# Sums of q and k by two engines instead of by transfers for three batches, and a re-planned order, in a two-scale attention kernel with a gated convolution

## The chip, the cores and the metric

The kernel runs on one core of a Trainium2 chip, as one program. The metric is the device time of one execution in microseconds (us); lower is better. Engine names: PE (TensorE matmul), PEld (its weight loads), DVE (VectorE), ACT (ScalarE), POOL (GpSimd), SP (SyncE, which issues most transfers).

## What is computed

Attention over 8 batches of 8 heads, 576 positions, 64 per head, at two scales that are added, then a convolution gate and two projections with 512 x 512 weights:

```
q_d, k_d, v_d = means of q, k, v over groups of 4 positions   # 144 rows
out_d   = softmax(q_d k_d^T / 8) v_d, repeated 4 times
out_loc = softmax(q k^T / 8 where |i - j| < 4) v
x       = out_d + out_loc, heads side by side                  # 576 x 512
gate    = sigmoid(sum over 5 taps of conv_w[k] * x shifted)
result  = (gate * (x @ w_val)) @ w_out
```

Softmax subtracts the row maximum and adds 1e-9 to the sum. Everything is float32; the projections run as three products of high and low parts (lines 1159 to 1161).

## The kernel before

The work is cut into 32 steps p, one for each batch b = p // 4 and pair of heads c = p % 4. A step has two arms. The local arm: `sl` (banded scores on PE, from the tile `qk` that SP loads), `mx`, `sub`, `exp`, `sum`, `rcp`, `norm` on DVE and ACT, `tl` (transposes on PE), their copy `pt` on ACT, and `x` (PE, with the loaded `vw`). The coarse arm: `sd` (PE, scores of sums over four positions, tile `qs`), `cmx`, `cbi`, three `cexp` with bias `cbi`, `cgrd`, `crcp`, `cnorm` on `pd` (DVE, ACT or POOL), `tc` (transposes), copy `pdt`, and `odp` (PE, with sums of v, tile `vs`; in batch 0 with v itself, tile `vg`), copied by ACT into `od`. DVE adds both into `xt` (lines 990). From `xt` come a high and a low part `xhs`, `xls`, and the gate `gp` with four taps on DVE (line 1070). The projections are cut into blocks j of 504 positions: `v{c}.{part}` and `o{c}.{part}` are pieces of three matmuls each; between them DVE gates (`h`), and ACT and DVE or POOL split it into `hhl`. An `out` block is scaled by ACT into one of two `ob` buffers (line 1251) and SP sends it (`out_t`). From step 8 on `sd` does two steps in one.

The sums over four positions of q and k come in one of two ways. `pool` (lines 720 to 746) adds them from the loaded `qk` on DVE or POOL: per step and for each of q and k an addition of 288 elements into `half` (line 733) and one of 144 into `qs` (line 734). `sums_in` (lines 653 to 689) loads the first of four position slices by SP, and POOL issues three transfers that add the others to it in memory (`accum_op`, line 669), each waiting for the one before. The constant `SUMB = 2` gives batches 0 and 1 to the engines, 2 to 7 to transfers. The sums of v for batches 1 to 7 always come by such transfers.

The order on all engines is made by `Planner`: every operation has a duration for each engine that may run it, a due time (`rank`, from a given order of PE's work and shifts in `SHIFT`), and `simulate` then runs a list schedule. Its start times are the order in which instructions are emitted; each engine then runs its list in order, waiting on semaphores only. `ORDER` is the head of PE's order, written as names; behind it `START`, `STEADY` and `DOUBLE` patterns go on (`tensor_order`). `EARLY` is the order of the first transfers on SP. `Transfers` models the queues of SP and POOL, `fetched` the loading of PE's code in pieces of 127 instructions. Matmuls on constants (line 627) keep PE running where the planner expects a gap. [...]

## Time and profile before

| what | value |
|---|---|
| median of 3 runs | 367.86 us (366.77 to 368.74) |
| the profiled execution's own time | 365.61 us |
| its span, first to last instruction | 363.8 us |
| mean granted TensorE clock | 0.999 |
| PE, DVE, ACT, POOL busy | 98%, 86%, 67%, 19% of the span |
| transfers | 69.01 MB; queue q0, POOL's accumulating ones, 17.50 MB |

The span is what the trace covers; 1.8 us of the profiled execution lie around it. "Busy" is the union of an engine's instructions, and a matmul's end is modelled, so that a busy PE may still lose time between two matmuls; idle time before an instruction, and what ended it, is shown in brackets.

### The profile page before, as it was taken

Reading aid. Unit: us, or ns where it says so; the run is one execution under the profiler, and the core shown is the slowest. Engines: PE = TensorE matmul, PEld = TensorE weight load, DVE = VectorE, ACT = ScalarE, POOL = GpSimd, SP = SyncE. Lnnn points to the kernel's source line nnn. Section 1 sums busy time; section 2 is a strip of 40 time slices with the busy share of each in tenths; the row PEclk is TensorE's granted clock in tenths of the full one; section 3 lists DMA queues with packets and bytes.
Section 4 is the critical chain, followed back from the end, with each engine's and each line's share of the span. In section 5 each row is a group of like instructions: output and inputs, shape, how many; then the busy total and the mean of one; then the engine's idle time right before and its main releaser. Section 6 shows DMA issues by size and latency. Waiting matters only on the chain.

```text
span 363.8 us, 14500 instructions
## 1 busy us (share of the span) xinstructions
PE 354.8 (98%) x6233; PEld 286.3 (79%) x6233; DVE 311.5 (86%) x696; ACT 244.1 (67%) x658; POOL 70.3 (19%) x95
## 2 busy tenths in 40 slices
PE   8899999999999999999999999999999999999996
PEld 5678776777877788888888887788878787878995
DVE  4999999999999699999999999999998996870520
ACT  2999998977687658784868577676767685422221
POOL 5013252622131123211312031202100110000000
PEclk9999999999999999999999999999999999999999
DMA  8999989999999977995699869992434012002012
GB/s 278 315 286 307 325 226 212 253 254 262 249 229 272 251 243 206 227 264 194 231 206 245 244 183 250 220 266 86 142 125 133 2 41 82 33 0 90 25 49 82
DMA packets 23152, 69.01 MB, mean 190 GB/s; under 512 B 2864, under 2 KB 8240, under 8 KB 23088
## 3 DMA queue, kind: packets, MB, share of 16 engines
q1 hardware_dynamic: 18192, 50.42, 41.6%
q0 software_dynamic: 4608, 17.50, 26.3%
q8 instruction: 49, 0.80, 1.0%
q10 hardware_dynamic: 288, 0.16, 0.2%
q14 instruction: 15, 0.12, 0.1%
HBM read 58.63 MB, written 9.44 MB: 187 GB/s over the span
## 4 chain that ended last, share of the span: by engine, by line
PE 78%; DMA 10%; ACT 6%; DVE 3%; issue 1%; POOL 0%; DVEq 0%; ACTq 0%; POOLq 0%
PE out L1159 9%; PE out L1161 8%; PE out L1160 8%; PE val L1159 8%; PE val L1161 8%; PE val L1160 8%; DMA vs<-in_vgr 7%; PE odp L1021 6%; PE x L979 5%; PE tl L929 5%; PE sl L772 5%; PE tc L952 5%; PE sd L849 3%; DMA out_t<-ob 2%; PE sl L758 1%
## 5 line engine op out<-in xcount | busy, mean ns | idle before, releaser
L1070 DVE SCALAR_TENSOR_TENSOR gp<-xt,cw,gp 128x576 f32<-128x576 f32 x128 | 103.4, 812 | 3.1 <-ACT gp L1064 2.4
L1159 PE MATMUL val<-xhs,wh_v 128*128 128x504 f32 (+1 forms) x160 | 63.0, 394 | 0.0
L1161 PE MATMUL val<-xls,wh_v 128*128 128x504 f32 (+1 forms) x160 | 59.5, 372 | 0.0
L1160 PE MATMUL val<-xhs,wl_v 128*128 128x504 f32 (+1 forms) x160 | 59.4, 371 | 0.0
L1159 PE MATMUL out<-hhl,wh_o 128*128 128x504 f32 (+1 forms) x144 | 58.6, 407 | 0.1
L1161 PE MATMUL out<-hhl,wh_o 128*128 128x504 f32 (+1 forms) x144 | 54.8, 381 | 0.0
L1160 PE MATMUL out<-hhl,wl_o 128*128 128x504 f32 (+1 forms) x144 | 54.7, 380 | 0.0
L872 ACT ACTIVATE pd<-sd,cbi 112x144 f32<-112x144 f32 x96 | 35.5, 387 | 7.8 <-DVE cbi L865 7.8
L1251 ACT ACTIVATE ob<-out 128x504 f32<-128x504 f32 (+2 forms) x40 | 22.1, 557 | 24.4 <-PE out L1161 15.3
L1207 POOL TENSOR_TENSOR hhl<-h,hhl 128x504 fp32r<-128x504 f32 (+1 forms) x17 | 19.3, 1138 | 98.8 <-ACT pt L934 41.9
L1187 DVE SCALAR_TENSOR_TENSOR h<-gp,val 128x288 f32<-128x288 f32 (+6 forms) x64 | 26.6, 445 | 12.8 <-PE val L1161 12.7
L959 ACT COPY pdt<-tc 72x336 f32<-72x336 f32 x64 | 25.5, 434 | 16.3 <-PE tc L952 16.1
L1201 ACT CAST hhl<-h 128x504 fp32r<-128x504 f32 (+2 forms) x44 | 22.0, 521 | 20.3 <-DVE h L1187 19.6
L1161 PEld LDWEIGHTS val<-xls,wh_v 128*128 128x128 f32 x160 | 30.1, 188 | 5.2
L1159 PEld LDWEIGHTS val<-xhs,wh_v 128*128 128x128 f32 x160 | 30.1, 188 | 4.6 <-issue 0.8
L1160 PEld LDWEIGHTS val<-xhs,wl_v 128*128 128x128 f32 x160 | 30.2, 189 | 3.6
L809 DVE TENSOR_TENSOR pexp<-ex,rs 64x350 f32<-64x350 f32 x61 | 31.6, 518 | 1.3
L1081 ACT ACTIVATE gp<-gp 128x576 f32<-128x576 f32 x32 | 22.2, 694 | 14.1 <-DVE gp L1070 14.1
L934 ACT COPY pt<-tl 128x256 f32<-128x256 f32 (+1 forms) x64 | 25.7, 430 | 8.7 <-PE tl L929 8.4
L1161 PEld LDWEIGHTS out<-hhl,wh_o 128*128 128x128 f32 x144 | 27.1, 188 | 5.5 <-DVE hhl L1207 0.4
L1159 PEld LDWEIGHTS out<-hhl,wh_o 128*128 128x128 f32 x144 | 27.1, 188 | 5.4 <-DVE h L1187 0.5
L1160 PEld LDWEIGHTS out<-hhl,wl_o 128*128 128x128 f32 x144 | 27.2, 189 | 3.4
(97 smaller groups left out, 711.9 us busy)
## 6 DMA issues: line engine op xcount, KB each, us to landing
qk<-in_qk SPq DMA_DIRECT2D x32, 586.0 KB, 6.1
qs<-in_qkr POOLq DMA_DIRECT2D x18, 576.0 KB, 7.7
vw<-in_vw SPq DMA_DIRECT2D x32, 320.0 KB, 5.4
out_t<-ob SPq DMA_DIRECT2D x32, 252.0 KB, 5.2
vs<-in_vgr POOLq DMA_DIRECT2D x21, 320.0 KB, 8.2
qs<-in_qkr SPq DMA_DIRECT2D x6, 576.0 KB, 6.6
vs<-in_vgr SPq DMA_DIRECT2D x7, 320.0 KB, 6.7
raw_v<-in_w_val SPq DMA_DIRECT2D x4, 512.0 KB, 5.5
```

Of the source, the lines that this page charges most:

```text
L809: return eng.tensor_tensor(out=px[r].rearrange("p (m b) k -> p b m k", b=2)[:, :, :, BQ * e : BQ * e + KW], in0=s["ex"][r].rearrange("p (b ...
L872: nc.scalar.activation(out=s["pd"][:, g], in_=s["sd"][:, g], func=AF.Exp, scale=1.0 / 128.0, bias=s["bi"][:, g : g + 1], accum_out=s["csm" ...
L934: nc.scalar.copy(out=s["pt"][:, lo : lo + n], in_=s["tl", u])
L959: nc.scalar.copy(out=s["pdt"][:, kb], in_=s["tc", kb])
L1070: return nc.vector.scalar_tensor_tensor(out=s["gp"], in0=s["xt"][:, k : k + S], scalar=cw[:, c, k : k + 1], in1=s["gp"], op0=ALU.mult, op1 ...
L1081: nc.scalar.activation(out=s["gp"], in_=s["gp"], func=AF.Tanh, scale=0.5)
L1159: nc.tensor.matmul(out=o, lhsT=wh[:, d, col], rhs=his[d], start=d == 0, stop=False)
L1160: nc.tensor.matmul(out=o, lhsT=wl[:, d, col], rhs=his[d], start=False, stop=False)
L1161: nc.tensor.matmul(out=o, lhsT=wh[:, d, col], rhs=los[d], start=False, stop=d == NC - 1)
L1187: nc.vector.scalar_tensor_tensor(out=t["h"][:, cs], in0=st[b * NC + c]["gp"][:, f:e], scalar=1.0, in1=box["o"][:, cs], op0=ALU.add, op1=AL ...
L1201: nc.scalar.copy(out=t["hh"][:, cuts[n]], in_=t["h"][:, cuts[n]])
L1251: nc.scalar.mul(t["ob"][:, cs], box["o"][:, cs], 0.5)
```

## The change

It has four parts. `SUMB = 2` becomes `SUMS = (2, 5)`: transfers sum q and k for batches 2 to 4 only, and batches 5 to 7 go to `pool`, on DVE or POOL. `EARLY`, `ORDER` and `SHIFT` hold other lists; `ORDER` now reaches to `tl0.14`, where it ended at `v0.0.2`. The planner's model of PE's code is a new one: a piece of code is called for some instructions ahead and, if an accumulating transfer is under way, comes after it; `pick_tensor` prefers, after 60 us, work whose code is not late. The planner's duration of `cbi` is 95 for 77, and an accumulating transfer counts as landed 2700 ns after its data, for 1600.

```
-SUMB = 2
+SUMS = (2, 5)
 EARLY = (
-    "qk.0 vw.0 qk.1 raw.0 vg.0 qk2.0 cwf.0 qk.2 vw.1 raw.1 vg.1 raw.2 qk.3 raw.3 vw.2 vg.2 vg.3 qk.4 vw.3 "
+    "qk.0 vw.0 qk.1 raw.0 vg.0 cwf.0 qk.2 vw.1 raw.1 raw.2 vw.6 qk.3 vw.5 vg.1 vg.2 vw.3 vw.2 raw.3 vg.3 "
...
 ORDER = (
...
-    "odp.11 x.10 x.11 tc1.12 v0.0.2"
+    "odp.11 x.10 tl1.12 x.11 tc1.12 tl0.12 v0.0.2 tl1.13 v0.1.2 v0.2.2 v0.3.2 tc0.13 v1.0.2 sl.13 v1.1.2 "
...
-    LANDING = 1600
+    LANDING, WRITTEN = 1600, 2700
...
-    FETCH = ((60000, 6000), (1e9, 4200))
+    CALL = ((60000, 0, 3650), (1e9, 12, 2300))
+    BRING, BEHIND = 2350, 1400
...
                     if t is not None and t <= now:
-                        return k
-                    if t is not None:
+                        late = now > 60000 and self.fetched(k, now, ops[k]["opts"]["PE"], now, dma, keep=False)
+                        if best is None or late < best[0] - 200:
+                            best = late, k
+                        if best[0] <= 200:
+                            return best[1]
+                    elif t is not None:
...
-            if nm == "qs" and b < SUMB:
+            if nm == "qs" and not SUMS[0] <= b < SUMS[1]:
                 continue
...
-        if p >= NC * SUMB:
+        if SUMS[0] <= p // NC < SUMS[1]:
             return
...
-            pooled = [("qe", x) for x in pairs] if p < NC * SUMB else [("qs3", p // NC)]
+            pooled = [("qe", x) for x in pairs] if not SUMS[0] <= p // NC < SUMS[1] else [("qs3", p // NC)]
...
-        op(("cbi", p), "DVE", 77, bias, [("cmx0", p)])
+        op(("cbi", p), "DVE", 95, bias, [("cmx0", p)])
...
+    def brought(self, call, dma):
+        t = call + next(x for until, _, x in self.CALL if call < until)
+        on = list(dma.added[-6:])
...
+        for begin, end in on:
+            if begin < call + self.BEHIND:
+                t = max(t, end)
+        return t + self.BRING
```

What this moves on the engines, at two places. The first is POOL's queue for batches 5 and 6 (`half20_0` is the first addition for q of step 20, `qs6` the tile of batch 6, `hhl3_1` the low part of block 3). Before:

```order
L1207 TENSOR_TENSOR hhl3_0_3409<-h3_0_3382,hhl3_0_3409 128x504
L1207 TENSOR_TENSOR hhl3_1_3482<-h3_1_3465,hhl3_1_3482 128x504
L1207 TENSOR_TENSOR hhl3_2_3590<-h3_2_3561,hhl3_2_3590 128x504
L669 DMA qs6_3493<-in_qkr 128x1152
L669 DMA vs6_3515<-in_vgr 80x1024
L669 DMA qs6_3493<-in_qkr 128x1152
L669 DMA vs6_3515<-in_vgr 80x1024
```

The same place now:

```order
L1246 TENSOR_TENSOR hhl3_0_3411<-h3_0_3384,hhl3_0_3411 128x504
L772 TENSOR_TENSOR half20_0_3491<-qk20_3360 128x288
L1246 TENSOR_TENSOR hhl3_1_3471<-h3_1_3467,hhl3_1_3471 128x504
L773 TENSOR_TENSOR qs5_3490<-half20_0_3491 128x144
L772 TENSOR_TENSOR half20_1_3560<-qk20_3360 128x288
L708 DMA vs6_3525<-in_vgr 80x1024
L773 TENSOR_TENSOR qs5_3490<-half20_1_3560 128x144
L773 TENSOR_TENSOR qs5_3490<-half21_0_3656 128x144
L773 TENSOR_TENSOR qs5_3490<-half21_1_3720 128x144
L708 DMA vs6_3525<-in_vgr 80x1024
```

The accumulating transfers of `qs6` are gone and additions for steps 20 and 21 stand between the low parts and the transfers of `vs6`. Counted over the whole program, of the 48 new additions DVE runs 8 into `half` and 7 into `qs`, POOL 16 and 17; DVE gives up 4 `cnorm` and 2 `norm` halves, ACT takes 3 `cnorm` more.

The second place is PE's queue at the third output block of block 1 (`out1_2`), whose result needs a free `ob` buffer; `out1_0` is the one that used it before. Before:

```order
L1161 MATMUL out1_2_2352<-hhl1_2_2056,wh_o_98 128x504
L929 MATMUL tl11_1_2378<-ident_77,pexp1_81 128x128 x2
L929 MATMUL tl10_0_2384<-ident_77,pexp0_80 128x128 x3
L1159 MATMUL out1_2_2352<-hhl1_3_2176,wh_o_98 128x504
L1160 MATMUL out1_2_2352<-hhl1_3_2176,wl_o_99 128x504
L1161 MATMUL out1_2_2352<-hhl1_3_2176,wh_o_98 128x504
```

Now (the first half of `sl12`, sixteen rows on the mask, is left out):

```order
L1200 MATMUL out1_2_2366<-hhl1_2_2076,wh_o_98 128x504
L968 MATMUL tl11_1_2392<-ident_77,pexp1_81 128x128 x2
...
L811 MATMUL sl12_2396<-qk12_1903 29x35 x40
L968 MATMUL tl10_0_2452<-ident_77,pexp0_80 128x128 x3
L1198 MATMUL out1_2_2366<-hhl1_3_2189,wh_o_98 128x504
L1199 MATMUL out1_2_2366<-hhl1_3_2189,wl_o_99 128x504
L1200 MATMUL out1_2_2366<-hhl1_3_2189,wh_o_98 128x504
```

The scores of step 12, which stood behind the block, now run before its last piece.

## Rows read from the trace of the kernel before

**Rows 1.** The page's first part: busy time, share of the span and instructions of each engine.

```profile
PE 354.8 (98%) x6233; PEld 286.3 (79%) x6233; DVE 311.5 (86%) x696; ACT 244.1 (67%) x658; POOL 70.3 (19%) x95
```

**Rows 2.** Busy time by stretch of the span: start and end in us, length, then for each engine busy us and count, granted clock, share of the DMA engines' time, GB/s.

```profile
10.00:50.00 40.00, 38.46 (x838) 29.78 (x839) 39.47 (x96) 37.51 (x103) 8.62 (x10) 1.00 0.97 302
50.00:100.00 50.00, 49.12 (x839) 37.50 (x838) 48.85 (x104) 39.24 (x106) 18.97 (x23) 1.00 0.99 243
...
170.00:290.00 120.00, 119.52 (x2330) 97.22 (x2329) 114.87 (x263) 84.37 (x238) 20.33 (x20) 1.00 0.65 178
```

**Rows 3.** The waits of PE over the whole span: who waited for whom, us in total, times, longest.

```profile
PE odp L1021 <- DMA vs<-in_vgr: 0.5, 1, 0.5
PE tl L929 <- ACT od L1031: 0.5, 1, 0.5
...
PE odp L1021 <- ACT pt L934: 0.4, 1, 0.4
PE odp L1021 <- issue: 0.4, 1, 0.4
```

**Rows 4.** The chain of waits that ended last, between 113 and 123 us: start, us, what.

```profile
113.55 0.59 ACT ob L1251
...
114.17 7.44 DMA out_t<-ob
...
121.69 0.59 ACT ob L1251
...
122.70 0.71 PE odp L1021 x8
```

**Rows 5.** The timeline of SP's queue, ACT and PE between 227 and 237 us: start, us, engine, line, operation, out<-in; in brackets idle time before it.

```profile
227.72 0.83 SPq L644 DMA_DIRECT2D out_t<-ob  x2
...
235.33 0.59 ACT L1251 ACTIVATE ob<-out 128x504 f32<-128x504 f32 x1 [1.15 <-PE x L979]
235.82 0.70 ACT L1031 COPY od<-odp 128x288 f32<-128x288 f32 x2
...
236.26 0.85 PE L929 MATMUL tl<-ident,pexp 128*128 128x128 f32 x5 [0.45 <-ACT od L1031]
```

**Rows 6.** The page's DMA issues: queue, count, KB each, median us from issue to landing.

```profile
qk<-in_qk SPq DMA_DIRECT2D x32, 586.0 KB, 6.1
qs<-in_qkr POOLq DMA_DIRECT2D x18, 576.0 KB, 7.7
...
out_t<-ob SPq DMA_DIRECT2D x32, 252.0 KB, 5.2
```

**Rows 7.** The additions into `half` and `qs` (duration in ns, least, median, most; first and last start), and two groups of DVE work (count | busy us, mean ns of one | idle before).

```profile
L733 DVE TENSOR_TENSOR half<-qk x12: 404/448/460, 4.9 to 49.9; 128x288 f32<-128x288 f32 x12
L734 DVE TENSOR_TENSOR qs<-half x10: 247/300/308, 5.4 to 60.5; 128x144 f32<-128x144 f32 x10
L734 POOL TENSOR_TENSOR qs<-half x6: 416/425/427, 6.3 to 57.3; 128x144 f32<-128x144 f32 x6
L733 POOL TENSOR_TENSOR half<-qk x4: 659/664/668, 7.5 to 59.7; 128x288 f32<-128x288 f32 x4
...
L809 DVE TENSOR_TENSOR pexp<-ex,rs 64x350 f32<-64x350 f32 x61 | 31.6, 518 | 1.3
...
L897 DVE TENSOR_TENSOR pd<-pd,crs 112x432 f32<-112x432 f32 x16 | 9.7, 613 | 0.2
```

**Rows 8.** DVE instructions that ran beside a POOL addition (timeline: start, us), and the spread of the same two forms over the span (ns, least, median, most).

```profile
67.36 1.07 DVE L865 TENSOR_SCALAR cbi<-cmx 112x3 f32<-112x3 f32 x1
...
172.14 1.03 DVE L1070 SCALAR_TENSOR_TENSOR gp<-xt,cw,gp 128x576 f32<-128x576 f32 x1
...
L865 DVE TENSOR_SCALAR cbi<-cmx x32: 146/155/1189, 8.5 to 289.0; 112x3 f32<-112x3 f32 x32
...
L1070 DVE SCALAR_TENSOR_TENSOR gp<-xt,cw,gp x128: 746/808/1157, 24.3 to 322.5; 128x576 f32<-128x576 f32 x128
```

**Rows 9.** The timeline where the load of `qk` for step 23 is issued by SP, and where the coarse scores of steps 22 and 23 run on PE.

```profile
190.72 0.64 SPq L644 DMA_DIRECT2D qk<-in_qk  x1
...
209.37 0.97 PE L849 MATMUL sd<-qs 64*64 64x144 f32 x24
```

**Rows 10.** The timeline of PE where it goes from a projection's piece to the scores of a step.

```profile
207.91 0.39 PE L1160 MATMUL val<-xhs,wl_v 128*128 128x504 f32 x1
208.14 0.40 PE L1161 MATMUL val<-xls,wh_v 128*128 128x504 f32 x1
208.47 0.27 PE L758 MATMUL sl<-mask_b,ident_b 64*32 64x175 bf16 x8
208.56 0.88 PE L772 MATMUL sl<-qk 64*29 64x35 f32 x80
```

**Rows 11.** The timeline of PE and ACT at the first coarse transposes of steps 4 and 5.

```profile
48.68 1.03 ACT L895 ACTIVATE pd<-pd,crs 112x144 f32<-112x144 f32 x3
48.77 0.35 PE L952 MATMUL tc<-ident,pd 112*72 112x112 f32 x2
...
49.45 0.60 PE L952 MATMUL tc<-ident,pd 112*72 112x112 f32 x2
```

**Rows 12.** The timeline where SP issues the load of v for step 1 (`vg`), and where PE first uses it.

```profile
11.16 0.33 SPq L644 DMA_DIRECT2D vg<-in_vg  x1
...
22.19 0.46 PE L1021 MATMUL odp<-pdt,vg 72*64 72x144 f32 x3
```

## The prediction

> **What bounds the kernel now.** I read the page's busy times first. PE is busy for 98% of the span, DVE for 86%, ACT for 67%, POOL for 19% [rows 1]: PE bounds the whole, and DVE comes near enough to bound a stage. The table by stretches says where. From 10 to 50 us PE is busy 38.46 of 40 us, DVE 39.47 and ACT 37.51, with the DMA engines at 97%; from 50 to 100 us PE has 49.12 of 50. From 170 to 290 us, the stage where batches 5 to 7 are worked on, PE has 119.52 of 120 us and DVE 114.87 [rows 2]. So nearly all that PE can win lies before 100 us, where DVE has no time to spare, and in a few holes behind. The list of PE's waits gives those holes their size: 0.5 us for the accumulated v, 0.5 for ACT's copy `od`, 0.4 for ACT's copy `pt`, 0.4 with no releaser ("issue") [rows 3].

> Two of the holes have one cause. At 113.55 us ACT scales an output block; its transfer takes 7.44 us; ACT stands until 121.69 before it may write that buffer again; the copy `pt` behind it in ACT's queue comes late, and PE starts `odp` at 122.70 [rows 4], after a hole of 0.4 [rows 3]. At 235.33 us it happens again: ACT had been idle for 1.15 us, the output transfers had been issued from 227.72 on, the copy `od` is queued behind, and PE loses 0.45 us [rows 5]. The row names `x` as the releaser there, but scaling an output block doesn't read it; the landing fits, 7.6 us after the issue. The median output transfer lands in 5.2 us [rows 6]. What both moments share is accumulating transfers in the air.

> **The change, part by part.** All terms are against the profiled execution's own 365.61 us; the median of the runs is 367.86, so 2.25 us higher, and I carry the difference over to it.

> *Transfers removed.* Batches 5 to 7 lose 3 plain loads and 9 accumulating transfers of 576 KB. The output transfer of 227.72 us then flies beside transfers of v alone, and at the median of 5.2 us it lands 2.4 us sooner, more than ACT's idle 1.15. PE's hole of 0.45 us closes: **-0.45**, bounds -0.45 and 0.

> *PE's order at block 1.* The transfers of batches 3 and 4 stay, so the output transfer of 114.17 us may stay long. But `sl` of step 12 now runs before the last piece of the third output block, so ACT asks for the buffer later by about the 0.88 us that such scores take (208.56 to 209.44 us, by the starts around it [rows 9, 10]). PE's own hole is 0.4: **-0.4**, bounds -0.4 and 0, since the copies behind ACT's wait could be wanted elsewhere.

> *Fewer steps down to small matmuls.* Behind a projection's piece a matmul of scores starts 0.33 us after the last big one, where a big one follows another in 0.23 [rows 10], so an entry costs 0.1. By PE's two lists there are 7 fewer entries from a `v` or `o` piece into `sl`, `sd`, `x` or `odp`, and 5 more from transposes, whose price no row shows; it lies between 0 and the same 0.1. So -0.7 to -0.2; I take **-0.4**.

> *The early transposes.* At 48.68 us the transposes of step 5 follow those of step 4 and wait, slice by slice, for ACT's three normalizing instructions: two of step 4 take 0.35 us together, two of step 5 0.60 [rows 11]. The change puts nine matmuls and `x` between. Some 0.6 us could go. But PE next needs the accumulated v of batch 1, for which it already waits 0.5 us [rows 3], and that chain of three transfers starts from the same place in SP's list. What PE saves at 49 us it waits for at 56: **0**, bounds -0.6 and +0.5 (the chain later, by the two additions that POOL now runs between its transfers).

> *First loads.* `vg` of step 1 moves behind a weight load of 512 KB and a `qk` of 586 KB, which at the 302 GB/s of that stretch [rows 2] is 3.6 us. Issued at 11.16 us before, it would land at 17.3 with `qk`'s median of 6.1 [rows 6] and now at about 20.9; PE uses it at 22.19 [rows 12]. Covered by 1.3 us: **0**, and up to +1 if the queue is slower. The fourth weight load moves back by three transfers, some 3 us; its first use is over 15 us later.

> *The planner's view of late code.* The 0.4 us of "issue" is the only wait of PE that has no other releaser [rows 3]. A plan that knows when code comes late has little to win here: **0**, bounds -0.4 and +0.5 for a new wait, since scores of steps 13 and 14 now run back to back.

> *The sums.* DVE runs 8 more additions of 0.448 us and 7 of 0.300, and gives up 4 `cnorm` of 0.613 and 2 halves of `norm` of 0.518 [rows 7]: 3.6 + 2.1 - 2.5 - 1.0 = +2.2 us. Its idle time from 170 to 290 us is 120 - 114.87 = 5.1 us [rows 2], which hides it, with 2.9 left. POOL runs 16 of 0.664 and 17 of 0.425, 17.8 us on an engine idle four fifths of the time, and loses 9 issues. Are the sums in time? `qk` of step 23 is issued at 190.72 us; with 6.1 us it lands at 196.8; the two additions for q and two for k take 2.2 us on POOL; the scores run at 209.37 [rows 9]. Ten us of cover, so a transfer of `vs` waited for in POOL's queue ahead of them (7.7 us for one of that kind [rows 6]) still fits. Three `cnorm` more on ACT lie beside work of other engines, since ACT has 84 of 120 us. **0**, if the additions leave DVE's instructions as they are.

> Sum: -0.45 - 0.4 - 0.4 = -1.25, so 364.4 for a profiled execution and **366.6 us** for the median.

> **The rivals.**

> *A, slower: the additions hold DVE up.* A `cbi` that met a POOL addition took 1.07 us, where the median is 0.155, and a tap 1.03 us against 0.808 [rows 8]. So a meeting costs 0.22 to 0.92 us, and I take the middle, 0.57. The stage where 33 more such POOL instructions run has 2.9 us of DVE idle left. For it: the stage holds most of the taps, and additions are tied behind one DVE instruction only. Against it: the plan keeps them apart, and the median tap and `cbi` have their short length although POOL runs low parts beside them already. From six meetings on PE waits; from eight (4.2 / 0.57) the kernel is slower than before. With eleven: 6.3 - 2.9 - 1.25 = +2.1, **370.0**. [...]

> *B, nothing is won.* Before 100 us DVE is busy 98 to 99% of the time [rows 2]; what PE saves there it waits for again, and the two holes behind ACT move to the next output block. Then **367.8**.

> *C, faster: the runs held more of these waits than the profiled execution.* The median lies 2.25 us above it. If that is output blocks and loads waiting beside accumulating transfers, half of it, 1.1 us, may go with those of batches 5 to 7: **365.5**. For it: a transfer took 7.44 us where the median is 5.2. Against it: no row of the other runs is there.

> **How the numbers follow.** About 0.5%, 1.84 us, is what a measurement can tell from no change. Forecast 0.50 (365.2 to 368.0: faster by over that 0.17, within it 0.32, slower 0.01), A 0.18 (slower 0.16, within 0.02), B 0.12 (within 0.11, slower 0.01), C 0.20 (all faster). So faster 0.37, same 0.45, slower 0.18. The range, 364.0 to 370.0, holds the forecast with its bounds, B, nearly all of C and half of A, and leaves out about 0.12.

> **What would show it.** Right: ACT's idle time before an output block near 120 and 235 us gone, and PE's waits for `pt` and `od` with it; DVE busy some 2 us more between 170 and 290 us, with `cbi` near 0.16 us and taps near 0.81; additions done 5 us or more before the scores that use them; PE's wait for `vs` near 56 us still there. Wrong: PE waiting for `qs`, or DVE instructions of batches 5 to 7 over 1 us (A); PE's gaps before 100 us shorter by over 1 us, which I gave nothing; or new "issue" waits near steps 13 and 14.

## The result, and the profile after

The changed kernel takes 369.35 us in the median (365.48 to 370.79), the kernel before beside it 367.44: ratio 1.0054, 95% interval 1.0034 to 1.0074. A second series gave 369.47 against 367.36, ratio 1.0089 [1.0044, 1.0135]. So it is slower, by some 2 us; the forecast was 366.6. The medians here and below are of all executions, while a ratio leaves out those over 1.5% above their kernel's fastest, so that it need not be the ratio of the two medians. The profiled execution took 370.2 us, with a span of 368.2.

The page's first part, two queues of its third and two rows of its last, after:

```profile
PE 357.0 (97%) x6236; PEld 289.2 (79%) x6236; DVE 313.0 (85%) x705; ACT 249.3 (68%) x667; POOL 82.1 (22%) x122
...
q0 software_dynamic: 3312, 12.19, 18.5%
q8 instruction: 49, 0.80, 1.0%
...
out_t<-ob SPq DMA_DIRECT2D x32, 252.0 KB, 2.4
...
qs<-in_qkr POOLq DMA_DIRECT2D x9, 576.0 KB, 7.7
```

The parts that the change meant to move did move: half of the accumulating transfers of q and k are gone, an output block lands in 2.4 us instead of 5.2 [rows 6], POOL has 12 us more work [rows 1]. Now the stretches that answer to [rows 2], and one more:

```profile
10.00:50.00 40.00, 36.53 (x692) 28.64 (x693) 34.94 (x83) 32.83 (x87) 8.83 (x11) 0.91 0.94 285
50.00:100.00 50.00, 48.94 (x966) 37.83 (x966) 49.15 (x109) 40.73 (x108) 16.83 (x20) 1.00 0.96 241
140.00:150.00 10.00, 9.70 (x234) 7.49 (x233) 9.26 (x24) 5.80 (x22) 4.04 (x4) 1.00 0.51 119
170.00:290.00 120.00, 119.88 (x2329) 97.61 (x2330) 117.94 (x274) 86.69 (x238) 32.45 (x48) 1.00 0.51 143
```

From 170 to 290 us PE is as busy as before, 119.88 of 120 us, and DVE is 3.1 us busier, with 2.1 to spare. From 10 to 50 us PE ran 692 matmuls instead of 838, at a granted clock of 0.91, and DVE and ACT, nearly full before, stood idle for 5 and 7 us. The waits of PE, which answer to [rows 3]:

```profile
PE tl L968 <- DVE pexp L848: 1.7, 2, 0.9
PE odp L1060 <- issue: 1.6, 1, 1.6
PE sl L811 <- issue: 1.0, 1, 1.0
...
PE x L666 <- ACT pd L911: 0.4, 1, 0.4
PE out L1198 <- DVE h L1226: 0.3, 1, 0.3
```

The waits for accumulated v, for `od` and for `odp`'s `pt` are gone. "issue", 0.4 us before, is now 2.6. PE's timeline shows its two places (columns as in [rows 10]; in brackets the wait):

```profile
22.26 0.47 PE L1060 MATMUL odp<-pdt,vg 72*64 72x144 f32 x4
24.32 3.62 PE L1060 MATMUL odp<-pdt,vg 72*64 72x144 f32 x28 [1.60 <-issue]
...
70.43 0.65 PE L811 MATMUL sl<-qk 64*29 64x35 f32 x52
72.05 0.35 PE L811 MATMUL sl<-qk 64*29 64x35 f32 x28 [0.97 <-issue]
```

Both stops are in the middle of a group whose operands are all there. What is missing, as I read the records of q8, is code. This queue, of kind `instruction` above, moves 49 transfers of 16 KB (0.80 MB), in before and after alike. Counted from the first, PE's pairs of weight load and matmul can be cut into blocks of 127 (the first has 94), which gives 49 ends as well, and every stop with no releaser of 0.15 us or more, in any trace here, stands 2 to 7 pairs behind the end of such a block: here behind the fourth of 32 `odp`, there behind the 52nd of 80 `sl`. For each end of a block there is one transfer of q8, which starts between 2 us before PE passes that end and 7 us behind it (2.5 and 8.5 in f4, below). That it brings the block after next is read from the stops, since no record names what a transfer holds: PE goes on 1.2 to 1.6 us after it has landed (before 1.43 at 23.01 us, after 1.39 at 24.32 and 1.29 at 72.05, f4 1.54 at 43.30). One stretch of the DMA view, 21.55 to 23.0 us, holds the transfer for the first stop, between loads of SP (from 17.0 to 21.55 us q8 moves nothing):

```profile
q1 hardware_dynamic: 154, 0.35, 91.7%
q8 instruction: 1, 0.02, 5.7%
```

By this reading the margin at each block is the time that PE takes for one block, less the time from a block's end until the code is there and those 1.2 to 1.6 us more. From the traces' records of q8 and of PE's starts, in us:

| profile | end of a block | code of the block after next lands | end of the next block | PE goes on |
|---|---|---|---|---|
| before | 17.00 | 21.58 | 22.20 | 23.01 |
| after | 17.04 | 22.93 | 22.26 | 24.32 |
| before | 62.15 | 64.35 | 66.42 | no stop |
| after | 65.88 | 70.76 | 70.81 | 72.05 |

At 70 us accumulating transfers were in the air from 59 to 72 us, and in the new order PE passes an end of a block, at 65.88, in their midst. That they delay the code isn't shown: in the kernel before such transfers ran from 62.2 to 67.4 us, and the code for the end at 62.15 landed 2.2 us behind it.

### The profile page after: what moved, and what is told of

It is laid out like the page before. It is cut to its first block, busy times and chain, and to the rows that moved or that the text cites. A ratio compares the mean times of both kernels' runs of the same rounds, so it can differ in the third digit from the quotient of the medians.

```text
span 368.2 us, 14558 instructions
## 1 busy us (share of the span) xinstructions
PE 357.0 (97%) x6236; PEld 289.2 (79%) x6236; DVE 313.0 (85%) x705; ACT 249.3 (68%) x667; POOL 82.1 (22%) x122
## 4 chain that ended last, share of the span: by engine, by line
PE 77%; DVE 13%; ACT 4%; issue 3%; DMA 1%; DVEq 0%; ACTq 0%
PE out L1198 8%; PE out L1199 8%; PE out L1200 8%; PE val L1198 7%; PE val L1200 7%; PE val L1199 7%; PE odp L1060 6%; PE sl L811 5%; PE tc L991 5%; PE x L1018 5%; PE tl L968 4%; DVE gp L1109 4%; PE sd L888 3%; DVE h L1226 1%; PE sl L797 1%
## 5 line engine op out<-in xcount | busy, mean ns | idle before, releaser
L1226 DVE SCALAR_TENSOR_TENSOR h<-gp,val 128x288 f32<-128x288 f32 (+6 forms) x64 | 26.6, 445 | 13.2 <-PE val L1200 12.9
L1246 POOL TENSOR_TENSOR hhl<-h,hhl 128x504 fp32r<-128x504 f32 (+1 forms) x18 | 20.1, 1118 | 75.7 <-DVE gp L1109 41.4
L1029 DVE TENSOR_TENSOR xt<-x,od 128x290 f32<-128x290 f32 x64 | 25.7, 446 | 9.3 <-PE x L1018 5.4
L848 DVE TENSOR_TENSOR pexp<-ex,rs 64x350 f32<-64x350 f32 x59 | 30.6, 518 | 1.3
```

The source lines that it names most:

```text
L848: return eng.tensor_tensor(out=px[r].rearrange("p (m b) k -> p b m k", b=2)[:, :, :, BQ * e : BQ * e + KW], in0=s["ex"][r].rearrange("p (b ...
L1029: nc.vector.tensor_tensor(out=s["xt"][:, 4:].rearrange("p (m a j r) -> p a m j r", m=NPR, a=2, r=2)[:, par], in0=s["x"][par].rearrange("p ...
L1226: nc.vector.scalar_tensor_tensor(out=t["h"][:, cs], in0=st[b * NC + c]["gp"][:, f:e], scalar=1.0, in1=box["o"][:, cs], op0=ALU.add, op1=AL ...
```

## Experiments

Theories: (1) the new order of the first loads makes PE's code late before 50 us; (2) PE's new order puts ends of blocks where code comes late; (3) the sums cost nothing. The rival to all was A of the prediction. Where "every list as it is" is said, the planner's choices were replaced by each engine's own list, written out, and only what the text names was altered.

### The sums

s1 and d2 are one kernel, run twice: before, with `SUMS = (2, 5)` and the three conditions on it, planned again. s4: after, with

```diff
-SUMS = (2, 5)
+SUMS = (2, 8)
```

s1: 

> The kernel before with only the sums of q and k for batches 5 to 7 on VectorE and GpSimd (PE's list is the same up to two entries). Theory 3 (the sums are hidden, and an output transfer that finds no accumulating transfers beside it lands sooner): the hole near 236 us gone, 0 to 0.7 us faster than before, 366.7 to 367.4. Rival (the additions on GpSimd hold VectorE up, or DVE runs out of idle time): 1 us or more slower than before, over 368.4, with VectorE's instructions of batches 5 to 7 longer or PE waiting for them.

d2: 

> The kernel before with only the sums of q and k for batches 5 to 7 on VectorE and GpSimd, once more beside the others, since it is the best so far: 0 to 0.4% faster than before if the sums gain what the holes behind output transfers cost, 365.9 to 367.4; the same as before if those holes are chance.

s4: 

> The changed kernel with the sums of q and k of batches 5 to 7 back on accumulating transfers (PE's list the same up to 11 entries behind 250 us). Theory 3: same as the changed kernel or up to 0.7 us slower, 369.3 to 370.0, with the hole near 236 us back. Rival (the sums cost the time): 1 to 2 us faster than the changed kernel, 367.4 to 368.4.

Measured: s1 366.21 us, ratio to before 0.9996 [0.9967, 1.0025]; d2 365.81, 0.9982 [0.9950, 1.0013]; s4 368.40, 1.0040 [1.0011, 1.0069]. By s1 and d2 the sums cost nothing; a gain isn't established. s4 alone would not decide it: its 368.40 lies at the edge of what the rival gave, not in the range of theory 3. In d2, 170 to 290 us reads

```profile
170.00:290.00 120.00, 120.00 (x2341) 97.85 (x2342) 117.02 (x276) 88.05 (x249) 32.83 (x47) 1.00 0.49 138
```

PE has no wait there, and DVE has the 117 us that the prediction worked out. s4, without the sums of batches 5 to 7 on engines, is still slower than before. The slowdown is elsewhere.

### The first loads

f1 and d1 (one kernel, run twice): before, every list as it is, but SP's first 18 loads; f2: after, with the opposite edit.

```diff
-... qk.2 vw.1 raw.1 vg.1 raw.2 qk.3 raw.3 vw.2 vg.2 vg.3 qk.4 vw.3
+... qk.2 vw.1 raw.1 raw.2 qk.3 vg.1 vg.2 vw.3 vw.2 raw.3 vg.3 qk.4
```

f1: 

> The kernel before, every engine's list of instructions as it was, except that SP issues its first 18 loads in the order of the change (raw_v third, qk of step 3 ahead of vg of step 1). Theory 1 (the new order of the first loads makes code and loads late for PE near 20 to 25 us): PE stops for 1 to 1.6 us at odp of step 1, where before the kernel stopped 0.4, in some executions with a stretch at half clock behind it: 1 to 2 us slower than before, 368.5 to 369.5. Theory 2 (the loss is all in PE's own new order, later): same as before, 367.4, stop of 0.4 or less.

d1: 

> The kernel before with SP's first 18 loads in the order of the change, once more, since the first runs gave 1.0038 [1.0006, 1.007] but a profile with no long stop near 24 us. Theory 1: 0.3 to 0.5% slower than before again, and in a second profile a stop or a stretch of lower clock between 10 and 50 us, where it loses 1 us more than before. Rival (the first runs were chance): within 0.2% of before.

f2: 

> The changed kernel, every engine's list as it is, except that SP issues its first 18 loads in the order of before. Theory 1: the stop at odp of step 1 shrinks from 1.6 to 0.4 us and the clock of 20 to 40 us is 1.0; 1.2 to 2 us faster than the changed kernel, 367.3 to 368.2, so about as before. Theory 2: same as the changed kernel, 369.3, with a stop of some 1.6 us still there.

Measured: f1 368.86 us, 1.0038 [1.0006, 1.0070]; d1 368.65, 1.0036 [0.9998, 1.0073]; f2 368.18, 1.0037 [1.0009, 1.0064]. So the loads alone cost some 0.37% (d1's interval just reaches 1), and f2, where they are the old ones, shows that the other new lists cost as much by themselves. That is what theory 1 said of the time, but mostly not of the place: in neither profile does `odp` stop for long at 24 us (f1 0.21 us), and a second profile of the changed kernel itself (a0, below) did not stop there at all. A place that recurs is 35 us, in the scores of step 5. In f1, and in a0:

```profile
34.64 0.23 PE L960 MATMUL sl<-qk 64*29 64x35 f32 x3
35.76 0.43 PE L960 MATMUL sl<-qk 64*29 64x35 f32 x33 [0.89 <-issue]
```

```profile
34.22 0.23 PE L811 MATMUL sl<-qk 64*29 64x35 f32 x5
35.16 0.85 PE L811 MATMUL sl<-qk 64*29 64x35 f32 x75 [0.71 <-issue]
```

Of eight profiles with the new loads (four in flight, blocks where they were) five wait there, 0.4 to 0.9 us, two others (after and f3) at 24 us, 1.6 us; of six with the old loads one waits at 35 us, 0.36 us, and none longer than 0.6 at 24. The block before ends at about 29 us, the next one 5.5 us later. From the end at 29 us until the code lands it takes 4.0 to 4.7 us in the six profiles with the old loads, 4.6 to 5.1 in the six with the new that had not stopped at 24 us. With the new order the four 512 KB loads `raw_o` are issued from 28.3 to 34.5 us in f1, from 28.1 to 32.3 in before: the code goes through beside them.

That these stops are the 0.37% isn't shown. Kernels with the old loads stop too: s1 for 0.72 us at 30 and for 1.00 us at 49 us, c2 (below) for 1.11 us at 18. The stop at 49 us, in the scores of another step, stands in four of the five profiles with the old list of PE and four loads in flight, 0.3 to 1.0 us, with either order of the loads. Here those of s1 and d1:

```profile
48.92 0.63 PE L772 MATMUL sl<-qk 64*29 64x35 f32 x49 [1.00 <-issue]
...
50.45 0.63 PE L960 MATMUL sl<-qk 64*29 64x35 f32 x49 [0.97 <-issue]
```

All stops for code ("issue", 0.15 us or more) before 60 us add up to 0 to 1.9 us in the six profiles with the old loads and to 0.4 to 2.1 in the eight with the new.

g2: f1 with fewer loads in flight; g3: s1 with the same edit; every list as it is.

```diff
-PACE = 4
+PACE = 3
```

g2: 

> The kernel before with the new order of the first 18 loads, and SP holding three loads in flight instead of four. Theory 1 (code for PE waits behind the loads that were issued ahead of it): the code of the block that ends at 29 us lands within 4.3 us of that end instead of 4.8 to 5.1, and the wait of step 5's scores at 35 us is gone; unless loads themselves come late, 0.2 to 0.4% faster than with four in flight, so as before. Rival (the code's delay has nothing to do with the loads in flight): 4.6 us or more, wait still there, time as with four or slower.

g3: 

> The kernel before with the sums of q and k of batches 5 to 7 on VectorE and GpSimd, the best so far (0.9996 and 0.9982 of before in two sessions), with three loads in flight instead of four. Theory 1: its waits for code before 60 us (0.6 to 1.9 us in two profiles) fall below 0.5 us, and it is 0.1 to 0.4% faster than before. Rival: with three in flight qk or vg come late before 60 us, where the DMA engines are 97% busy, and it is 0.3% or more slower than before.

Measured: g2 372.15 us, 1.0143 [1.0104, 1.0181]; g3 373.00, 1.0142 [1.0102, 1.0181]. Neither waits for code in step 5, and the code lands 3.4 us (g2) and 2.6 us (g3) behind the end of that block. But these ends come later, at 31.7 and 33.6 us, and with four loads in flight the code for an end at 33.7 us, in the changed kernel's profile, landed 2.5 us behind it. The first seven blocks together say more: the code landed 3.5 us behind their ends in the mean in g2, where it was 5.1 and 4.9 in f1 and d1, and 2.8 in g3, where it was 5.0 and 4.2 in s1 and d2. So fewer loads in flight go with sooner code. The time is that of g3's rival: PE waits for ACT and DVE instead. That late loads are behind these waits isn't shown: DVE's additions wait for `qk` 8.9 us in g2 (6.0 in f1), but 5.5 in g3 (4.9 in s1). The largest waits of g2:

```profile
PE tc L815 <- ACT pt L1122: 1.7, 2, 1.5
PE tl L1117 <- ACT pdt L1147: 1.6, 1, 1.6
PE x L815 <- DVE ex L975: 1.0, 1, 1.0
PE sd L1037 <- DVE xt L1178: 0.8, 1, 0.8
```

### The ends of blocks

a0 is the changed kernel itself. f4 has 48 pairs more at the start:

```diff
+        for _ in range(52 if plan.warm == 12 else 0):
+            nc.tensor.matmul(out=bank[0:32, 0:8], lhsT=ones(64, 32), rhs=ones(64, 8), ...)
-        for _ in range(plan.warm):
+        for _ in range(8 if plan.warm == 12 else plan.warm):
             nc.tensor.matmul(...)
```

a0: 

> The changed kernel as it is, beside the three below. All theories: 368.8 to 369.8, some 0.5% above before. A second profile tells a stop that belongs to the kernel from one that this execution had by chance: PE's loss from 140 to 150 us (1.4 us, 1.0 more than before) should stand in every profile, since there two blocks of 127 of PE's load and matmul pairs end 3.2 us apart, while the code for the block after next arrives 4.3 to 5 us after a block's end; the 1.6 us at 24 us may not.

f4: 

> The changed kernel, every engine's list as it is, with 48 more load and matmul pairs on PE at the very start (52 of 8 columns in place of 4 of the 12 warm-up matmuls of 350 columns), while PE waits for its first data; so each block of 127 pairs ends 48 pairs earlier in the work. By the trace's start times, ends of blocks then lie 1.5 us apart at 38 us, 1.2 us at 134 us, 3.7 at 78 us, 4.1 and 4.2 near 31 and 33 us. Theory 2: with 4.8 us from the end of a block to the arrival of the code for the block after next, 6.3 us more are lost than in the changed kernel, at those places: 373 to 376. Rival (blocks of code have nothing to do with the stops): the time as the changed kernel's, 369 to 370.5.

Measured: a0 369.47 us, 1.0089 [1.0044, 1.0135]; f4 377.24, 1.0282 [1.0228, 1.0335], 7.8 us more than a0 beside it, just above the 376 expected. The added pairs run while PE had nothing to do, and the first scores start at 5.24 us, as in the changed kernel (5.23). f4's stops stand at ends of blocks: at three of the places worked out beforehand (38, 78 and 134 us by the changed kernel's trace, later here by the stops before them; at 78 us 1.06 us are lost), and at 8 us, which the expectation had not listed:

```profile
7.91 0.63 PE L1013 MATMUL sl<-qk 64*29 64x35 f32 x50
11.59 0.35 PE L1013 MATMUL sl<-qk 64*29 64x35 f32 x30 [3.05 <-issue]
...
39.32 0.91 PE L868 MATMUL tc<-const-bfloat16-1.0 128*72 128x336 bf16 x5
43.30 0.29 PE L1193 MATMUL tc<-ident_s,pd 112*72 112x112 f32 x1 [3.06 <-ACT a_o L1349]
...
138.66 0.77 PE L1013 MATMUL sl<-qk 64*29 64x35 f32 x65
141.21 0.29 PE L1013 MATMUL sl<-qk 64*29 64x35 f32 x15 [1.78 <-issue]
```

The row of 43.30 names ACT's `a_o`, which is not read there; blocks end at 37.69 and 39.20 us, the code lands at 41.76, PE goes on 1.5 us later. So there the releaser in the bracket hides a wait for code. Every other engine's list is the same in f4, so it is shown that here the place of the blocks' ends alone cost 7.8 us.

### PE's order behind 118 us, and at 70 us

In every profile with the whole new list of PE, 140 to 150 us loses 1.3 to 1.6 us beyond what its matmuls take (how that is reckoned stands below, with the other stages; the expectations have 1.4 to 1.6 by slightly other prices); with the list of before, 0.3 or less. Two blocks end 3.2 us apart there; in the changed kernel's profile the code lands 2.3 and 3.6 us behind these two ends, where a0's expectation had 4.3 to 5; at the first seven ends of before it was 3.8 to 5.1. f3 gives PE its old order for steps 13 to 15, with ACT, DVE and POOL planned again; f5 in addition the old loads, planned again too; c1 moves six entries with every other list as it is; c2 also `sl.7` behind two pieces, with the old loads; g1 adds 8 pairs of 8 columns at 118 us.

```diff
 f3, f5: PE's list from v0.1.2 on as in the kernel before
 c1, c2:
-odp.12 odp.13 v3.2.2 tl1.14 v3.3.2 o0.0.2 x.12 x.13
+v3.2.2 v3.3.2 o0.0.2 odp.12 odp.13 tl1.14 x.12 x.13
 c2:
-o0.0.0 tc1.6 sl.7 o1.0.0 o0.1.0
+o0.0.0 tc1.6 o1.0.0 o0.1.0 sl.7
```

f3: 

> The changed kernel with PE's list for steps 13 to 15 as before the change (scores of steps 13 and 14 no longer back to back); SP's list is unchanged, ACT, DVE and GpSimd planned again. The ends of PE's blocks of code then lie 5 us or more apart at 135 to 150 us. Theory 2 (PE's new order brings ends of blocks nearer together than code arrives): the loss from 140 to 150 us falls from 1.4 to 0.5 us; 0.7 to 1.2 us faster than the changed kernel. Rival (the loss there comes from the changed work of DVE and ACT): 1.2 us or more is still lost there, the time as the changed kernel's.

f5: 

> The changed kernel with PE's list for steps 13 to 15 and SP's first 18 loads both as before the change. Theories 1 and 2 together: 1.7 to 2.5 us faster than the changed kernel, as before or up to 0.3% faster than it, 366.5 to 367.6. If only PE's list counts: as the kernel with that list alone; if neither: as the changed kernel.

c1: 

> The changed kernel, every engine's list as it is, but that three pieces of projections (nine matmuls) run between the scores of step 15 and the products of steps 12 and 13 instead of behind them. The two ends of code blocks near 141 and 144 us then lie 5 us apart instead of 3.2. Theory 2: the loss of PE from 140 to 150 us, 1.4 to 1.6 us in the four profiles with that order, falls to 0.5 to 0.8; 0.6 to 1.0 us faster than the changed kernel. Rival (the loss there comes from something else in steps 12 to 15): 1.3 us or more still lost, the time as the changed kernel's.

c2: 

> As the kernel before this one, and in addition two pieces of output projections ahead of the local scores of step 7 (the ends of code blocks near 66 and 71 us then lie some 6 us apart instead of 4.9) and SP's first 18 loads in the order of before. Theories 1 and 2: no wait for code in the scores of step 7 (0.4 to 1.5 us in three of four profiles); 1.5 to 2.5 us faster than the changed kernel, as before or up to 0.3% faster than it. Rival (scores that start 1.4 us later make DVE late, which has no time to spare before 100 us): the wait for code goes, and the transposes of step 7 wait for DVE instead; as the kernel before this one.

g1: 

> The changed kernel, every engine's list as it is, with 8 more load and matmul pairs of 8 columns on PE at 118 us, so that from there on each block of code ends 8 pairs earlier in the work; the ends near 141.1 and 144.3 us come to lie some 4.5 us apart instead of 3.2. If the loss from 140 to 150 us (1.4 to 1.6 us) is code: it falls to 0.9 or less, and the time by 0.3 to 0.7 us against the changed kernel. If it is the chain of copies on ACT and DVE in steps 12 to 15: 1.3 us or more is still lost there and the time is the changed kernel's, or up to 0.4 us more for the pairs.

| | us | ratio to before | lost from 140 to 150 us |
|---|---|---|---|
| f3 | 373.23 | 1.0144 [1.0068, 1.0221] | 1.8 |
| f5 | 371.25 | 1.0143 [1.0086, 1.0200] | 1.3 |
| c1 | 372.05 | 1.0142 [1.0084, 1.0200] | 3.2 |
| c2 | 370.82 | 1.0085 [1.0051, 1.0119] | 3.2 |
| g1 | 370.98 | 1.0107 [1.0065, 1.0148] | 1.5 |

All five missed: none is faster than the changed kernel. Planning the other engines again brought new waits (f3 and f5: `out <- DVE h`, up to 1.5 us). c1 made `odp` 2 us later, counted from the scores of step 15; ACT copies it (`od`) ahead of the exponentials `pd` of steps 14 and 15 in its list, and `x`, which follows them, waited:

```profile
146.06 0.81 PE L1212 MATMUL x<-pt,vw 64*64 64x58 f32 x40
148.12 1.32 PE L1212 MATMUL x<-pt,vw 64*64 64x58 f32 x40 [1.25 <-ACT pd L1105]
```

In g1 the ends lie 4.5 us apart as meant, but the code came 4.1 us after the first instead of 2.3, and two starts of `odp` still lay 0.57 us apart. So at 143 us two starts of `odp` at a block's end lie 0.24 to 0.69 us apart in four of the five profiles with the new order of steps 12 to 15. In the fifth, a0, they do not, and it loses as much: late code is not the larger part here. In after, a0, s4 and f2 some 0.3 to 0.5 us more are lost where an output piece follows transposes (at 150.03 us in the changed kernel's profile, behind DVE's `h`). How the rest divides stays open.

At 70 us the scores of step 7 stop for code in six of eight profiles with that order (0.28 to 1.74 us), in none of five with the order of before. c2, which moved them, does not stop there, but its copies then make it wait 1.05 us for DVE at 68 us: the rival of that expectation.

## Why the prediction was wrong

PE's time beyond what its matmuls take, by stage (worked out from PE's starts: each time between two starts, less the mean of its kind over the nine profiles of the table, outliers left out; matmuls on constants count as lost; us, mean and spread):

| stage | old lists, old loads (before, s1, d2) | old lists, new loads (f1, d1) | new lists, old loads (f2) | new lists, new loads (after, a0, s4) |
|---|---|---|---|---|
| 20 to 50 | 12.3 (12.0 to 12.6) | 12.6 (12.3 to 12.9) | 11.3 | 13.4 (12.5 to 14.8) |
| 50 to 80 | 1.6 (1.5 to 2.0) | 2.0 (1.9 to 2.1) | 2.8 | 2.8 (2.4 to 3.4) |
| of it, matmuls on constants | 0.1 | 0.7 | 0.5 | 1.2 |
| 80 to 140 | 2.5 (2.2 to 3.0) | 2.4 (1.7 to 3.0) | 1.4 | 1.8 (1.2 to 2.8) |
| 140 to 150 | 0.1 (0.0 to 0.3) | 0.2 (0.1 to 0.3) | 1.3 | 1.5 (1.3 to 1.6) |

Against before the last column has +1.1, +1.2, -0.8 and +1.4 us, and +0.2 in all other stages, together some +3.0, as the spans of these profiles (366.8 in the mean against 363.8); the medians of the two series say +1.9 and +2.1. The +1.2 from 50 to 80 us is time of matmuls on constants: three more are in the list, and some that ran at 48 us before now run past 50.

Stops for code, named by "issue", add up to 0.4, 2.5 and 0.6 us over the whole span in before, s1 and d2, to 2.1 and 2.5 in f1 and d1, to 1.9 in f2 and to 2.6, 1.1 and 2.1 in after, a0 and s4. So profiles of one kernel differ as much as the kernels do, and the means (1.2 old, 1.9 new) account for 0.7 of the 3.0 us directly. That the two new lists cost the time is shown by f1, d1 and f2; that late code can cost it, by f4; how much of it late code is, stays open.

- *The planner's view of late code*, put at 0 with bounds -0.4 and +0.5, and with it the order of PE, is the first step that failed. The prediction took the 0.4 us of "issue" [rows 3] for all there was to win or lose. It was the remainder of a margin that one execution of before happened to keep (s1, with PE's list the same up to two entries, stops for 2.5 us): a new order of 6,236 pairs moves every end of a block behind 33 us. Measured: with the old loads, f2, the new lists cost 0.37%, some 1.4 us, where all terms without the loads had come to -1.25. Of that, the stop for code at step 7 is 0.3 to 1.7 us in six of eight profiles, and `odp` at 143 us up to 0.6. The prediction did name new "issue" waits as a sign against it, near steps 13 and 14; the larger one came at step 7.
- *First loads*, put at 0 and up to +1, is the second: 0.37%, some 1.4 us, in f1 and d1. The price was asked of `vg` alone. `vg` itself was in time in f1 and d1, as worked out [rows 12] (in g1 `odp` waited 0.65 us for it, at 23.5 us); PE's code, which no row of [rows 6] lists and which takes time of the same 16 DMA engines as the loads (after, 21.55 to 23.0 us: q8 5.7%, q1 with the loads 91.7%), landed 4.6 to 5.1 us behind the end at 29 us instead of 4.0 to 4.7. How much of the 1.4 us that is stays open.
- *The two holes behind ACT* (-0.45 and -0.4): gone in the changed kernel's profile, and output blocks land in 2.4 us, as in s1 and d2 (s4, with the transfers, 4.6). The hole of 0.4 at 122.70 us stands in three of the five profiles with the old list of PE (s1 and d1 below; not in f1 and d2) and in none of after, a0, s4 and f2, so it was real, but of some executions. The one at 236.26 us stands in no other profile with the accumulating transfers of before (f1, d1); s4 has one like it, 0.79 us, at 201 us. A hole of one execution was counted as one of every execution.

```profile
123.35 0.71 PE L1021 MATMUL odp<-pdt,vs 72*64 72x144 f32 x8 [0.42 <-ACT pt L934]
...
125.21 0.71 PE L1209 MATMUL odp<-pdt,vs 72*64 72x144 f32 x8 [1.03 <-ACT pt L1122]
```

- *Fewer entries* (-0.4): not seen. By the same reckoning the matmuls that are not on constants take 325.2 us in either list.
- *The early transposes* (0): with the old loads 20 to 50 us lost 11.3 us, 1.0 less than before, in one profile. PE now waits for `pexp` near 40 us (0.5 to 1.3 us in all profiles with the new lists) where it waited for `pdt` (0.3 to 0.7). The wait for accumulated v near 56 us, forecast to stay, is gone in the changed kernel's profile and 0.9 us in s4.
- *The sums* (0): right, and rival A is refuted. The signs it asked for are not there: `cbi` and taps keep their median lengths [rows 8], and PE waits for nothing of DVE from 170 to 290 us.

```profile
L904 DVE TENSOR_SCALAR cbi<-cmx x32: 151/159/973, 8.5 to 292.3; 112x3 f32<-112x3 f32 x32
...
L1109 DVE SCALAR_TENSOR_TENSOR gp<-xt,cw,gp x128: 755/808/1192, 24.3 to 326.8; 128x576 f32<-128x576 f32 x128
```

  A's two prices were read beside the wrong instructions. The `cbi` of 67.36 us and the tap of 172.14 us [rows 8] ran beside high and low parts on POOL; the additions of sums end at 60.5 us in that kernel [rows 7]. POOL before, at these times:

```profile
66.17 1.55 POOL L1140 TENSOR_TENSOR wl_o<-a_o,wh_o 128x512 fp32r<-128x512 f32 x1
67.48 0.92 POOL L1207 TENSOR_TENSOR hhl<-h,hhl 128x252 fp32r<-128x252 f32 x1
...
171.31 1.25 POOL L1207 TENSOR_TENSOR hhl<-h,hhl 128x504 fp32r<-128x504 f32 x1 [11.59 <-DVE gp L1070]
```

  In the changed kernel's profile eleven of the two kinds met an addition, as many as A reckoned with: six `cbi` of 0.15 to 0.24 us, but for one of 0.73 that met a low part too, and five taps of 0.80 to 0.85. The longer `cbi`, 0.53 to 0.97 us, and a tap of 1.19 ran beside POOL's parts and normalizations, 0.8 to 1.4 us long. All `cbi` together took 8.7 us, 1.1 more than before, all taps 103.5, 0.4 less. Against the median of 0.159 us, six `cbi` beside POOL's long instructions took 0.4 to 0.8 us more, three others beside such instructions 0.16 to 0.29 us in all; taps beside additions show next to nothing of it (819 ns in the mean, 808 for the others). What holds the six up isn't shown.
- *Rival C* (half of the 2.25 us between median and profile goes): didn't come; the changed kernel's medians lie further up. For the transfers by themselves the intervals of s1 and d2 leave room for it (up to 0.3 and 0.5%).

Lower clocks stand behind the long stops. In the changed kernel's profile the 28 `odp` behind the stop of 1.60 us are 3.62 us long, where 29 took 2.05 before, and 20 to 30 us have a granted clock of 0.72, with 0.50 from 25 to 28; in f4 the stretches of 10 to 20 and 40 to 50 us, with the stops of 3.05 and 3.06 us, have 0.83. Over the timed executions, the mean granted clock was below 0.997 in 8 of 92 of the kernel before, 1 of 24 with the sums alone, 7 of 24 with the new loads alone, 17 of 34 of the changed kernel; its executions above that have a median of 368.3 us, those below 370.2, and those of before above it 367.0. So some 1.3 us of the slowdown stand without a lower clock. That the stops cause the lower clock is my estimate from this order in time (after: stop to 24.32 us, 0.50 from 25 us on); no run shows it.

The best kernel of the study is before with the sums alone (s1, d2): not slower than before, and not shown to be faster.

## What to carry to other kernels

PE is busy here for 97 to 98% of the span and runs 6,233 to 6,236 short pairs, and its code, as read from q8, came in 49 transfers beside the loads. In these traces a wait of 0.15 us or more in the middle of a group whose operands are ready ("issue") stood each time 2 to 7 pairs behind the end of a block of 127, and it came and went between executions of one kernel (1.60 us at 24 us in after, none there in a0). So read such a wait as a margin (time that a block takes, less time until its code has landed and PE goes on), not as a cost to be counted once; whether another kernel has such blocks, its own trace has to show. Here a new order of PE moved every end of a block behind 33 us, and the new lists cost 0.37% without the new loads (f2); the new loads alone cost 0.37% too (f1, d1), with code that landed 4.6 to 5.1 us behind the end at 29 us instead of 4.0 to 4.7. Look at both before pricing such a change at nothing. And before a hole is booked as a gain, look whether it stands in more than one execution: that of 0.4 us at 122.70 us stood in three of five profiles with the old list of PE.
